# A new order of work for a two-layer block on one core, with every scaling of the K and Q features on GpSimd

## The chip, the core and the metric

The kernel runs on one core of a Trainium2 chip. The core has five engines with a queue of their own each: TensorE (PE in the profile; its weight loads are PEld), VectorE (DVE), ScalarE (ACT), GpSimd (POOL) and SyncE (SP), which here only issues transfers. An engine takes its instructions strictly in the order of its queue, and waits at an instruction until the semaphores that it names have come. The metric is the time of one execution in microseconds (us); less is better.

## The reference

The input x has 2048 tokens of 640 numbers. Two residual layers follow each other.

```python
h  = x + A(layernorm(x))
h2 = h + B(layernorm(h))
# A: 32 heads of 20
q, k, v = split(x @ wqkv)
phi(t)  = concat(softmax(t @ w_phi[h]), softmax(-(t @ w_phi[h])))     # 40 features
kv, z   = sum_s phi_k[s] v[s]^T,  sum_s phi_k[s]
o       = phi_q @ kv / (phi_q . z + 1e-6)
A       = o @ wo
# B: F = 1536
B       = ((x @ w_gate) * (x @ w_up)) @ w_down
```

So layer A is a linear attention: all tokens' K features must have been summed (kv and z) before the first token's numerator can be formed.

## The kernel before

The tokens lie in 16 tiles of 128. Every step of every tile is an operation with a name, a key, an engine and, for a tile of a pool, the slots that it takes. All this stands in the table PLAN (lines 48 to 142), one entry `name:key:choice:slots` per operation. `arrange` sorts each engine's operations by key, and that order is the engine's queue; the keys are used for nothing else. The choice picks the engine where an operation has two (0 the first, 1 the second). `emit` then works out which earlier operations each one has to wait for. Nothing is decided while the kernel runs, so the order of each queue is the table's.

The steps, with their names (t is the tile) and lines:

- Start: GpSimd fills constants (gl, gla, glb: a mask GL, lines 325 to 336; id0 and id1: the identity, 324 and 327; eps, va1, phz, ekz, rqz, Sz, mk0 to mk2). TensorE runs ten products of zeros, warm0 to warm9 (365). Ph0 to Ph2 (374) spread w_phi over the heads. WT0 to WT4 (386) turn the K weights on TensorE, WTe copies them, F1_0 to F1_4 (405) fold w_phi into them and Fe1 copies the result; the Q weights come turned by transfers (wqt) and are folded as F0 and Fe0. The loads are named x0, x1, x2, ... (x, some two tiles at a time), wk, wv, wo, wg, wu, wd.
- First layer norm: L1s and L1a on VectorE (422 to 425) give the mean and variance, L1l and L1e on ScalarE (430, 433) the factor, L1n (437) a bias for those tiles that ScalarE normalises, xn (445, 447) the normalised tile on VectorE or ScalarE. xt turns it: tiles 0 to 3 on TensorE (456) with a copy xte, the others by a transfer on SP (465).
- V, K and Q (476): ten products of 320 (or 300 and 340) columns into two banks of PSUM, 16 tiles each. Ve copies V out (245). For K, Kx (488) takes exp of both signs on ScalarE, Ks (492) sums each group of 20 on VectorE, Kr and Ke (495, 497) form the reciprocals on ScalarE, Kn (512) scales the 1280 features by them, and KV (520) adds the tile to the sums kv and z on TensorE, eleven products.
- For Q, Qx (545, 547) takes the exponentials, Qs (550) the sums, Qr (553), Qb (557) and Qe (560) form the ratio of the two sums of a head, Qn (564) scales half of the features, 660 columns, and qT (569) turns the tile by a transfer on SP.
- After the last KV, KVe0 and KVe1 on VectorE (527) copy kv and z out under a mask. Then for each tile N (582) forms numerator and denominator on TensorE, dd, rd and o (593, 596, 599) divide on VectorE, oT (603) turns o by a transfer, O (609) multiplies by wo, h (615) adds x, hc (623, 624) centres the result, L2q (626), L2v (630) and L2r (633) form the second layer norm's factor, and hT (637) turns the tile.
- Layer B goes by five groups of 2, 4, 4, 4 and 2 tiles (0 to 4; group 4 is the last two tiles). U_b_f_0 and U_b_f_1 (652) are the gate and up products of the f-th 128 columns, five products each; g (657) copies the gate on ScalarE, u (660) multiplies on VectorE; D (671) is the down projection, y (683) scales and adds h, and w (685) stores. The last tile's D is cut into three parts of 320, 192 and 128 columns.

Kn and Qn, the scalings, and Qb may run on GpSimd (choice 0) or on VectorE (choice 1). This is how Kn is written:

```python
G.op("pool", "Kn%d" % t, lambda e, eng, ek=ek, sr=sr: e.tensor_tensor(
    out=T["ek"][:, ek.slots[0], 0:2 * D].rearrange("p (h f) -> p h f", f=DH),
    in0=T["ek"][:, ek.slots[0], 0:2 * D].rearrange("p (h f) -> p h f", f=DH),
    in1=T["SR"][:, sr.slots[0], 1, :].unsqueeze(2).to_broadcast([P, 2 * H, DH]), op=ALU.mult),
    pool_c(1280), LP, [ek, sr], [ek], kk, alts=[("dve", dve_c(1280), LD)])
```

Of the kernel before, what the change touches and what calls it, by code (L numbers as in the profile page):

```python
# [48 lines left out]
gl0:0.78 gla4:0.942 gla1:1.084 glb1:1.313 gla0:1.452 gla3:1.594 gla2:1.736 glb2:1.965 va1:2.104 eps:2.934 zero:0.91 warm0:1.239 warm1:1.665 warm2:2.091  # L49
warm3:2.517 w5:0.78:1 x0:0.78:1 Ph1:2.585:1 glb4:2.964 ekz:3.103 warm4:2.943 L1s0:3.188 L1a0:4.098 x1:1.26 L1s1:4.207 wk0:1.74:1 L1l0:4.331 L1e0:4.657  # L50
xn0:4.994::0 warm5:3.369 wk2:2.22:1 id0:3.337 id1:3.575 warm6:3.795 warm7:4.221 WT0:4.647::0 glb3:3.82 WTe0:5.506:1 warm8:5.266::1 warm9:5.481 xt0:5.696::1
WT2:5.974::2 L1a1:5.914 L1l1:6.147 L1e1:6.473 xte0:6.173:1 Ph2:4.048 glb0:4.642 Ph0:4.87 F1_0:6.391::3 Fe1_0:6.909:1 wk3:2.7 WT3:6.71::5 WTe3:7.492:1 wk1:3.18
WT1:7.128::6 x2:3.66 wk4:4.14:1 x3:4.62:1 xn1:6.711::1 xt1:7.545::7 xte1:8.078 wv2:5.1:1 x6:5.58 WTe2:7.223:1 F1_2:7.824::0 Fe1_2:8.662:1 wv0:6.06:1
WT4:8.143::3 x4:6.54 WTe1:7.747 F1_1:8.559::4 Fe1_1:9.245 F1_3:8.879::6 Fe1_3:9.829 L1s2:8.155 wv1:7.02 K0_0:9.422::0 WTe4:8.942:1 F1_4:9.694::2 L1s3:9.35
L1a2:10.137 L1a3:10.26 K1_0:10.012::4 wv3:7.5 K1_1:10.284 K1_2:10.555 K1_3:10.825 V0_0:11.097::6 Fe1_4:10.414:1 L1s6:10.369 x10:7.98 L1s4:11.25 wv4:8.46:1
K1_4:11.367 L1l2:10.998 L1e2:11.323 Kx1_0:11.838::0 Kx1_1:12.421 L1a6:12.037 L1n2:11.604 K0_1:11.639 K0_2:11.909 K0_3:12.181 K0_4:12.451 Kx0_0:13.005::1
L1s7:12.146 V1_0:12.723::2 wqt4:8.94 V0_1:12.993 L1n3:11.828 V0_2:13.264 xn3:12.933::2 V0_3:13.536 wqt0:10.25 xn2:13.589:1:3 xt3:13.806::4 V1_1:14.085
V1_2:14.357 L1s5:13.445 V0_4:14.627 L1a4:14.232 x8:11.56 V1_3:14.899 Kx0_1:14.395 L1a7:14.341 L1a5:14.45 L1l4:14.979 L1e4:15.305 x14:15.398:1 xte3:14.559:1
Ve0:15.877::0 L1s11:14.967 xt2:15.169::5 xte2:16.462 V3:15.448::0 L1n5:15.754:1 xn5:15.908::0 xt5:16.533 L1n6:15.585 L1n4:15.809 V1_4:16.805 Ve1:17.274::1
xn4:16.42::1 xt4:17.843 Ks0:16.932::0 K3:17.076::6 L1s9:18.325 K2:18.431::4 wqt2:19.153 Kr0:18.444 Ke0:18.735 Ve3:18.881::2 L1a11:19.112 L1n7:16.032  # L60
xn7:19.465:1:2 xt7:20.463 Kx3_0:20.27::2 Kx3_1:20.854 L1a9:19.235 Ks1:19.344::1 Kr1:21.438 Ke1:21.729 Kx2_0:21.875::3 Kx2_1:22.459 L1s10:20.737 xn6:21.524::3
xt6:22.149 V2:19.788::2 K5:21.143::0 Kx5_0:23.043::4 Kx5_1:23.627 L1s8:22.036 V4:22.5::6 Ve2:24.211::3 L1a10:22.823 Ks2:23.195::2 Kr2:24.795 L1a8:24.588
K4:23.855::4 Ve4:24.941::4 L1l8:25.525 L1e8:25.851 Kn0:19.069 KV0:25.212::0,1 Ks3:24.697::3 Kn1:22.063 KV1:25.544 V7:25.878::2 K6:27.233::6 wqt3:23.459
Kx4_0:25.944::1 L1n9:26.131 xn9:26.433::0 L1n8:26.355 xn8:26.945::1 Kr3:26.528 Kx4_1:26.674 V6:28.59::4 wqt1:24.769 Ke2:27.258 Ve7:27.433::5 wg1:26.079
Ke3:28.017 Kx6_0:28.79::0 wo0:26.559 x12:27.039 F0_1:29.945::2 phz:26.579 Kn2:27.592 Kx6_1:29.373 xt9:27.519 Sz:29.905 Kn3:30.084 Ve6:30.145::6 Ks5:27.457::0
Kr5:30.73 L1s15:28.85 L1n11:29.637:1 xn11:29.791::2 Ke5:31.02 K7:30.265::6 KV2:31.62 rqz:32.397 Ks6:30.303::1 Kn5:32.434 Fe0_1:31.166 Ks4:31.696::2
Kx7_0:32.151::3 V5:31.953::4 Kx7_1:32.736 L1s14:33.089 L1a15:33.876 L1s13:33.985 xt8:28.829 Ve5:33.51::7 wg2:30.139 F0_3:33.309::2 L1a14:34.772 L1n10:34.881:1
xn10:35.035::3 KV3:33.629 L1s12:35.547 L1a12:36.457 Kr4:34.093 Ke4:34.385 Kn4:34.747 Fe0_3:34.531 Kr6:35.114 V8:33.962::6 Ve8:35.517::0 K9:35.318::4
F0_0:36.673::2 Kx9_0:36.873::2 Kx9_1:37.458 Ke6:38.041 wd0:30.619 K8:36.992::6 F0_2:38.349::4 L1a13:36.566 Fe0_2:38.865 Fe0_0:37.191:1 L1l12:39.45 L1e12:39.776
L1n15:40.056 KV4:38.667 Ks7:37.931::3 Kx8_0:39.868::1 wg0:31.099 F0_4:39.001::2 L1n14:40.014:1 Fe0_4:40.059:1 KV5:39.319 xt11:31.579 Kx8_1:40.453 L1n13:40.798:1  # L70
K11:39.653::4 Kx11_0:41.209::4 Kr7:41.792 Kx11_1:41.938 xn13:40.953::0 Ke7:42.523 Q0_0:41.008::2 wd2:32.889 Q3:41.281::6 wu2:33.369 Qx3_0:42.846::0 Qx3_1:43.456
L1n12:41.465:1 Kn6:40.279 xt10:35.66 wg4:36.97 Ks8:41.51::0 Kr8:44.066 Kn7:42.856 Ke8:44.356 Q0_1:42.648 Q0_2:42.919 Q0_3:43.191 Q0_4:43.464 xn15:42.903::1
wu4:37.45 xt15:43.528 wo2:44.502:1 wg3:44.837 KV6:43.736 V9:44.069::4 Q1_0:45.425::6 wu0:45.318 Q1_1:45.697 Q1_2:45.968 xt13:45.797 Ks9:43.414::2 Kr9:44.983
Kn8:45.169 xn14:44.807::2 Qx0_0:45.129::1 Qx0_1:45.739 wu1:47.108 Qs3:45.319 Ke9:46.349 Kn9:47.483 Q1_3:46.24 Q1_4:46.513 Qx1_0:46.983::2 Ks11:46.755::1
KV7:46.785 Ve9:47.593::1 xn12:48.148::3 xt12:48.773 Qx1_1:48.176 Qs1:48.971 Kr11:48.786 Q9:47.117::2 Qs0:50.407 Qx9_0:48.932::3 Qx9_1:49.542 KV8:48.484
K10:48.818::4 Kx10_0:50.373::0 Kx10_1:50.958 Ks10:51.842::3 xt14:50.083 Qr0:51.959::0 Qb0:52.303 K15:50.173::6 Kx15_0:52.105::3 KV9:51.529 Qr1:52.69::1
Qb1:53.033 Qs9:53.234 Kx15_1:52.836 Qe1:53.419 mk0:53.233 Ke11:53.538 wu3:51.392 wd1:51.873 V10:51.862::2 Qn1:53.727 Ve10:53.684::3 Kr10:54.269 Kn11:54.992
V11:53.218::4 Ve11:54.775::2 Ks15:54.669::0 K13:54.575::6 Qr9:55.358::2 Qb9:57.304 qT1:55.062::0 Qe0:55.505 Qr3:55.623::3 Qb3:56.062:1 Ke10:55.77 Kn10:56.163:1
Kr15:56.181 Kx13_0:56.328::1 Kx13_1:56.911 Ks13:58.33::2 Ke15:57.495 K12:55.931::2 Kx12_0:57.642::2 Kx12_1:58.225 Kn15:57.83 Qn0:59.722:1 Q2:57.286::4
Qx2_0:58.852::4 Qx2_1:59.462 qT0:60.7::1 Q4:58.654::6 Kr13:60.072 Ke13:60.362 Qe3:60.508 Qn3:60.816 qT3:62.191::2 Qx4_0:60.627::5 Qx4_1:61.237 Qs2:60.572  # L80
KV10:60.02 Qs4:62.032 Qr2:62.126::1 Qb2:62.469 V12:60.353::2 Ve12:62.272::4 Ks12:63.468::3 Qe2:62.855 Qe9:62.974 Qn2:64.861:1 K14:61.709::4 Qn9:63.282
qT9:64.617::3 Kx14_0:63.266::0 Kx14_1:63.849 Qr4:64.433::0 Q13:63.066::6 Qx13_0:64.63::2 Qx13_1:65.24 Kr12:65.85 Ke12:66.141 Kn13:64.546 Q5:64.433::2
Ks14:65.71::1 Qx5_0:66.287::1 Qx5_1:66.897 V14:65.799::4 Ve14:67.507::7 Qb4:66.859 Qe4:68.091 Kr14:68.21 Ke14:68.501 qT2:66.55::4 Qs5:67.692 Qr5:69.246::3
Kn12:67.058 V13:67.156::6 Ve13:69.391::6 Q10:68.511::2 Qn4:69.127:1 Qx10_0:70.076::0 KV11:69.879 Qs13:69.978 V15:70.212::4 Kn14:69.371 Qx10_1:70.686 Qs10:71.481
KV12:71.567 KV13:71.9 Ve15:71.767::5 KV14:72.234 KV15:72.567 mk1:71.684 mk2:72.029 KVe0:73.097 Q6:72.9::6 qT4:70.106::5 KVe1:73.686 N1:74.266::2 Qb5:72.299
Qe5:72.575 Qn5:72.882 Qr13:72.694::2 Qb13:74.147 Qe13:74.421 dd1:74.797::0 rd1:75.013 Qr10:74.54::1 N3:74.6::4 qT5:74.79::0 o1:75.415::0 oT1:76.343::0
Qn13:74.728 qT13:77.653::2 Qx6_0:74.686::3 Qx6_1:75.296 dd3:76.227::0 rd3:76.442 o3:76.844::1 oT3:79.142::1 Q7:74.933::0 Qx7_0:76.498::4 Qx7_1:77.108 Qs7:77.903
N0:76.299::6 Q11:76.632::2 dd0:79.338::0 rd0:79.552 o0:79.956::2 Qx11_0:78.198::5 Qx11_1:78.808 Qr7:79.456::0 Qb7:79.799 Qe7:80.075 N2:77.999::4 oT0:80.882::2
Qb10:80.766:1 Q14:78.332::0 Qx14_0:80.194::1 Qx14_1:80.803 Q8:79.7::2 Qx8_0:81.862::2 Qx8_1:82.472 dd2:80.867::0 rd2:81.082 o2:81.484::0 O1:81.067::6 h1:82.624
Qe10:83.082 Qn7:80.382 qT7:82.192::1 N9:82.424::0 dd9:83.424::0 oT2:83.683::3 hc1:83.558::1 Q12:82.757::4 Qx12_0:86.403::4 Qx12_1:87.013 L2q1:87.623 rd9:83.638  # L90
o9:84.041::1 Qn10:83.389 N5:84.124::2 dd5:84.853::0 rd5:85.067 o5:85.471::2 O0:84.457::6 h0:86.281 L2q0:88.483 hc0:87.216:1:0 oT9:84.993::0 hT1:86.302
O3:85.816::0 hT0:87.79 N4:87.174::2 dd4:87.704::0 Q15:87.507::6 h3:87.811 rd4:88.611 qT10:89.099::4 Qs6:88.894 Qr6:90.448::3 Qb6:90.791 O2:88.874::4 h2:90.43
# [820 lines left out]
```

## Time and profile before

| | |
|---|---|
| time before, median of three runs | 275.81 us (275.66 to 277.15) |
| the profiled execution | 275.82 us |
| its span in the profile | 274.1 us |
| TensorE busy | 265.9 us, 97% |
| VectorE busy | 173.0 us, 63% |
| ScalarE busy | 121.3 us, 44% |
| GpSimd busy | 67.9 us, 25% |
| granted TensorE clock | 1.00 of full speed |

In the first 80 us VectorE is busy for 73.8 us, and GpSimd does 54.2 of its 67.9 us there. Matmuls are pipelined and the profile models their ends, so that a group starts 0.16 us before the modelled end of the one in front of it when nothing keeps it waiting; a wait shows as a later start. The number behind L is the line of the kernel. In a row of the timeline the bracket holds the time in which the engine was idle in front of the instruction, and the operation that ended it. In the chain that ended last, each row is one stretch of work on the path to the last instruction.

### The profile page before, as it was taken

To read this page: it belongs to the slowest core of one execution; us is meant where nothing else is said; L and a number is where in the kernel's file an instruction comes from. 1 tells how busy PE (TensorE), PEld (TensorE's weight loads), DVE (VectorE), ACT (ScalarE), POOL (GpSimd) and SP (SyncE) were. 2 spreads that over 40 slices of the span, in tenths; PEclk is the share of its full clock that TensorE was granted. 3 is DMA by queue.
4 is the path that set the end of the run, shared out by engine and by line. 5 is a ranking of instruction groups with operands and counts; after the bars stand their busy time and mean duration, and the time that the engine had idled before them with its cause. 6 is when DMAs were issued, how large, how long until landed. Compare 5 with 4: busy or idle time off the path is not lost.

```text
span 274.1 us, 5191 instructions
## 1 busy us (share of the span) xinstructions
PE 265.9 (97%) x2103; PEld 176.5 (64%) x2103; DVE 173.0 (63%) x310; ACT 121.3 (44%) x299; POOL 67.9 (25%) x88
## 2 busy tenths in 40 slices
PE   7999999999879999999999999999999999999996
PEld 2777787777556688856666676757544466544674
DVE  4999989999989998785984445231323331344314
ACT  2989878998747565322336144111213020004000
POOL 7026959498942104232000000000000000000000
PEclk9999999999999999999999999999999999999999
DMA  6985999967558979567436400027000000010003
GB/s 183 315 178 110 232 330 216 246 197 118 94 82 157 145 159 139 114 124 144 58 72 128 42 0 2 6 66 122 0 29 4 0 0 26 25 60 0 26 0 103
DMA packets 66600, 27.76 MB, mean 101 GB/s; under 512 B 57744, under 2 KB 65296, under 8 KB 66576
## 3 DMA queue, kind: packets, MB, share of 16 engines
q1 hardware_dynamic: 65760, 26.45, 46.1%
q10 hardware_dynamic: 816, 0.98, 1.3%
q8 instruction: 16, 0.26, 0.4%
q14 instruction: 8, 0.07, 0.1%
HBM read 11.00 MB, written 2.62 MB: 50 GB/s over the span
## 4 chain that ended last, share of the span: by engine, by line
PE 81%; DVE 13%; ACT 3%; POOL 1%; issue 1%; DVEq 0%; ACTq 0%; POOLq 0%
PE ps L652 38%; PE ps L671 19%; PE ps L476 13%; PE ps L609 7%; DVE S L550 5%; DVE SR L492 3%; DVE ph L564 2%; PE ps L582 2%; ACT ph L545 1%; PE ps L520 1%; PE ps L405 1%; DVE RQ L557 1%; DVE o L599 1%; DVE ek L512 1%; ACT Wp L245 0%
## 5 line engine op out<-in xcount | busy, mean ns | idle before, releaser
L652 PE MATMUL ps<-xnT,Wgu 128*128 128x512 bf16 (+1 forms) x600 | 107.5, 336 | 0.0
L652 PEld LDWEIGHTS ps<-xnT,Wgu 128*128 128x128 bf16 x600 | 58.3, 98 | 42.3 <-DVE ev L660 0.4
L476 PE MATMUL ps<-Wp,xnT 128*128 128x320 bf16 (+1 forms) x480 | 69.1, 299 | 0.7 <-DVE o L599 0.4
L657 ACT ACTIVATE gt<-ps 128x512 bf16<-128x512 f32 (+1 forms) x60 | 29.2, 510 | 90.6 <-PE ps L652 65.9
L660 DVE TENSOR_TENSOR ev<-ps,gt 128x512 bf16<-128x512 f32 (+1 forms) x60 | 33.3, 580 | 43.5 <-PE ps L652 26.8
L476 PEld LDWEIGHTS ps<-Wp,xnT 128*128 128x128 bf16 x480 | 45.0, 97 | 18.4 <-ACT ph L547 0.7
L671 PE MATMUL ps<-Wd,ev 128*128 128x320 bf16 (+2 forms) x396 | 54.0, 295 | 0.0
L671 PEld LDWEIGHTS ps<-Wd,ev 128*128 128x128 bf16 x396 | 38.0, 98 | 15.7 <-DVE ev L660 0.3
L683 DVE SCALAR_TENSOR_TENSOR Wp<-ps,rs,x_all 128x640 bf16<-128x640 f32 (+3 forms) x18 | 14.5, 808 | 41.2 <-PE ps L671 41.1
L512 POOL TENSOR_TENSOR ek<-ek,SR 128x1280 bf16<-128x1280 bf16 x15 | 36.1, 2418 | 4.2 <-ACT SR L497 4.2
L545 ACT ACTIVATE ph<-ps 128x600 bf16<-128x600 f32 x32 | 21.2, 676 | 6.5 <-PE ps L582 3.4
L550 DVE TENSOR_REDUCE S<-ph 128x66 f32<-128x1320 bf16 x16 | 23.9, 1512 | 0.3 <-ACT ph L547 0.2
L609 PE MATMUL ps<-Wo,Wp 128*128 128x320 bf16 x160 | 23.7, 299 | 0.2 <-ACT ph L547 0.2
L492 DVE TENSOR_REDUCE SR<-ek 128x64 f32<-128x1280 bf16 x16 | 23.4, 1470 | 0.2 <-ACT ek L488 0.2
L488 ACT ACTIVATE ek<-ps 128x640 bf16<-128x640 f32 x32 | 20.9, 699 | 1.8 <-PE ps L476 1.4
L564 POOL TENSOR_TENSOR ph<-ph,RQ 128x660 bf16<-128x660 bf16 x13 | 17.5, 1355 | 10.5 <-ACT RQ L560 10.3
L609 PEld LDWEIGHTS ps<-Wo,Wp 128*128 128x128 bf16 x160 | 15.3, 98 | 7.1 <-issue 0.7
L626 ACT ACTIVATE ek<-x_all,mv 128x640 bf16<-128x640 bf16 x16 | 13.2, 824 | 10.9 <-DVE x_all L615 10.7
L630 POOL TENSOR_SCALAR ln<-mv 128x1 f32<-128x1 f32 x11 | 2.1, 192 | 58.2 <-ACT ek L626 57.7
L615 DVE SCALAR_TENSOR_TENSOR x_all<-ps,x_all 128x640 bf16<-128x640 f32 x16 | 13.1, 819 | 4.5 <-PE ps L609 4.5
L599 DVE TENSOR_TENSOR o<-ps,sm 128x720 bf16<-128x720 f32 x16 | 14.4, 902 | 0.7
L245 ACT ACTIVATE ev<-ps 128x640 bf16<-128x640 f32 x16 | 11.4, 710 | 0.9 <-PE ps L476 0.4
(67 smaller groups left out, 172.3 us busy)
## 6 DMA issues: line engine op xcount, KB each, us to landing
out_dram<-Wp SPq DMA_DIRECT2D x15, 160.0 KB, 1.8
Wgu<-in_B_w_gate_dram SPq DMA_DIRECT2D x5, 384.0 KB, 5.0
Wd<-in_B_w_down_dram SPq DMA_DIRECT2D x4, 480.0 KB, 5.0
Wgu<-in_B_w_up_dram SPq DMA_DIRECT2D x5, 384.0 KB, 6.5
x_all<-in_A_x_dram SPq DMA_DIRECT2D x5, 320.0 KB, 5.5
ev<-in_A_wqkv_dram SPq DMA_DIRECT2D x5, 160.0 KB, 3.4
Wp<-in_A_wqkv_dram SPq DMA_DIRECT2D x5, 160.0 KB, 5.2
x_all<-in_A_x_dram SPq DMA_DIRECT2D x3, 160.0 KB, 3.8
```

Of the source, the lines that this page charges most:

```text
L476: ins = e.matmul(pb(b, hb)[:, 0:n1 - n0], lhsT=T["xnT"][:, NC - 1 - c, P * t:P * (t + 1)], rhs=T["Wp"][:, POS[kind], c, n0:n1], start=(c = ...
L488: G.op("act", "%sx%d_%d" % (nm, t, s), lambda e, s=s, b=b, ek=ek: e.activation(out=T["ek"][:, ek.slots[0], 0:2 * D].rearrange("p (b h s f) ...
L492: G.op("dve", "%ss%d" % (nm, t), lambda e, ek=ek, sr=sr: e.tensor_reduce(out=T["SR"][:, sr.slots[0], 0, :], in_=T["ek"][:, ek.slots[0], 0: ...
L512: G.op("pool", "Kn%d" % t, lambda e, eng, ek=ek, sr=sr: e.tensor_tensor(out=T["ek"][:, ek.slots[0], 0:2 * D].rearrange("p (h f) -> p h f", ...
L545: e.activation(out=v[:, 0:10].rearrange("p (b g) j f -> p b g j f", b=2), in_=pp(b, 0, 300).rearrange("p b (g j f) -> p b g j f", j=3, f=D ...
L550: G.op("dve", "Qs%d" % t, lambda e, t=t, ph=ph: e.tensor_reduce(out=T["S"][:, t, 0:66].rearrange("p (g k) -> p g k", k=6), in_=pv(ph).rear ...
L564: return e.tensor_tensor(out=v, in0=v, in1=T["RQ"][:, rq.slots[0], 1, 0:33].rearrange("p (g j) -> p g j", j=3).unsqueeze(3).to_broadcast([ ...
L609: ins = e.matmul(pb(b, hb)[:, 0:320], lhsT=T["oT"][:, oT.slots[0], c, :], rhs=T["Wo"][:, c, 320 * hb:320 * (hb + 1)], start=(c == 0), stop ...
L652: ins = e.matmul(pb(b)[:, 0:n], lhsT=T["Wgu"][:, gu, c, P * ft:P * (ft + 1)], rhs=T["xnT"][:, NC - 1 - c, o0:o0 + n], start=(c == 0), stop ...
L657: G.op("act", "g%d_%d" % (bi, ft), lambda e, pg=pg, gt=gt, n=n: e.activation(out=T["gt"][:, gt.slots[0], 0:n], in_=pb(pg)[:, 0:n], func=AF ...
L660: o_ = G.op("dve", "u%d_%d" % (bi, ft), lambda e, pu=pu, gt=gt, hh=hh, ft=ft, n=n: e.tensor_tensor(out=T["hh"][:, hh.slots[0], ft, 0:n], i ...
L671: ins = e.matmul(pb(b, hb)[:, 0:w], lhsT=T["hh"][:, hh.slots[0], ft, P * tt:P * (tt + 1)], rhs=T["Wd"][:, ft, c0 + w * hb:c0 + w * (hb + 1 ...
```

## The change

Only the table PLAN differs. No operation is added or taken away: both tables have the same 1018 entries. The ten products of zeros and the four tiles (0 to 3) whose x is turned on TensorE are in both. What differs are the order of every queue, many slots, and the engine of some operations:

- Kn10, Qn0, Qn2, Qn4, Qb3, Qb10, Qb11 and Qb14 go from VectorE to GpSimd, so that all Kn, Qn and Qb are there.
- The biases L1n5, L1n10, L1n12, L1n13 and L1n14 go from VectorE to GpSimd, L1n7 the other way. Ph1 goes from VectorE to GpSimd, in front of the second half of the identity (id1).
- xn3, xn4, xn6, xn8 and xn10 go from VectorE to ScalarE, xn2 the other way. The copies Ve2, Ve10, Ve11, Ve13, Fe0_2, Fe0_3 go from ScalarE to VectorE, Fe0_0 and Fe0_4 the other way; WTe0, WTe1, WTe2 and xte0 go to ScalarE, WTe3, xte1, xte2 and Fe1_2 to VectorE. Some hc and L2v of the second layer norm change engines too.
- On SP, x1 and x0 now stand first, w5 goes to ScalarE's queue. wu1 and wg4 (384 KB each) and x12 are loaded early, in front of x8, x10 and wqt0. wd0 and wd2 are issued from ScalarE, x0, x14 and wo2 no longer are.
- On TensorE, warm8 and warm9 stand with the other eight; the order of the V, K and Q groups is another (Q7 comes before the first numerator N1, Q2 and Q4 and others change places), and the products of groups 0, 1 and 4 of layer B are mixed otherwise with the numerators and O. Kn15 is the last K scaling instead of the fourth from the end.
- The end of the queue is nearly the same: D14, D10, D12, D11, D13, D15_1.

The entries that the text speaks of, one to a line (all others change their keys too):

```diff
-Kn10:56.163:1
+Kn10:55.445
-Qn0:59.722:1
+Qn0:57.957
-Qn2:64.861:1
+Qn2:69.554
-Qn4:69.127:1
+Qn4:65.312
-Qb3:56.062:1
+Qb3:47.539
...
-Kn15:57.83
+Kn15:70.819
-L1n10:34.881:1
+L1n10:24.5
-Ph1:2.585:1
+Ph1:4.778
-id1:3.575
+id1:5.17
...
-xn4:16.42::1
+xn4:18.632:1:1
-xn6:21.524::3
+xn6:17.39:1:0
-Ve10:53.684::3
+Ve10:51.962:1:3
-Ve11:54.775::2
+Ve11:57.97:1:2
...
-x8:11.56
+x8:11.21
-x10:7.98
+x10:11.69
-wu1:47.108
+wu1:8.94
-wg4:36.97
+wg4:9.42
...
-Q6:72.9::6
+Q6:69.966::6
-Q7:74.933::0
+Q7:74.354::0
-N1:74.266::2
+N1:75.721::6
```

## The prediction

> **What bounds the kernel now.** I read the page first (engine shares, slices), then TensorE's timeline, the chain that ended last, and GpSimd's timeline against VectorE's. In each timeline row the columns are start, duration, what it is, and in brackets the idle time in front and who ended it.
>
> ```profile
> PE 265.9 (97%) x2103; PEld 176.5 (64%) x2103; DVE 173.0 (63%) x310; ACT 121.3 (44%) x299; POOL 67.9 (25%) x88
> ```
> TensorE is busy for 97% of 274.1 us, so a new order can win only what TensorE waits. Its timeline, from 66 us on:
> ```profile
> 65.81 3.70 PE L476 MATMUL ps<-Wp,xnT 128*128 128x300 bf16 x26
> 69.68 1.54 PE L476 MATMUL ps<-Wp,xnT 128*128 128x300 bf16 x10 [0.17 <-ACT ph L547]
> ...
> 74.42 0.51 PE L520 MATMUL ps<-ev,ek 128*128 128x63 bf16 x11 [0.50 <-POOL ek L512]
> 75.31 0.51 PE L520 MATMUL ps<-ev,ek 128*128 128x63 bf16 x11 [0.39 <-ACT ev L245]
> 75.67 1.53 PE L476 MATMUL ps<-Wp,xnT 128*128 128x300 bf16 x10
> 78.83 0.85 PE L582 MATMUL ps<-KVm,scratch 128*128 128x63 bf16 x22 [1.63 <-DVE KVm L527]
> ```
> Between 10.03 us (K0's first product) and 69.5 nothing waits: each group starts 0.16 before the last one's modelled end. Then come waits in front of Q10, KV13, KV14, KV15, N1, Q12 and O2: 0.17, 0.16, 0.50, 0.39, 1.63, 0.43 and 0.23, with the lost overlap 4.6 us. After O2 there is none. A count agrees: with 1.36 us per ten-product group, 0.33 per K'V or numerator, 1.08 and 0.545 per five gate/up products, 3.26 per down projection (pieces of the chain), the work after 10.03 is 256.6; the last product ends at 271.51, so 4.9 us are lost.
>
> Who makes TensorE late? The chain, 49.8 to 78.8 us, is VectorE throughout:
> ```profile
> 54.17 1.44 DVE S L550
> 55.61 1.39 DVE SR L492
> 57.00 1.27 DVE RQ L557
> 58.27 1.50 DVE ek L512
> 59.77 1.40 DVE SR L492
> 61.16 1.52 DVE ph L564
> 62.68 2.87 DVE S L550 x2
> 65.56 1.39 DVE SR L492
> 66.95 2.69 DVE ph L564
> 69.64 1.40 DVE SR L492
> 71.04 1.43 DVE S L550
> 72.47 2.60 DVE ph L564
> ```
> These are reductions (L492, L550), four scalings (L512, L564: Kn10 1.50, Qn0 1.52, Qn2 2.69, Qn4 2.60) and one small subtraction (L557: Qb3 1.27), the five together 9.6 us. They are long because of GpSimd:
> ```profile
> 58.70 3.28 POOL L512 TENSOR_TENSOR ek<-ek,SR 128x1280 bf16<-128x1280 bf16 x1 [0.28 <-ACT SR L497]
> 61.95 1.91 POOL L564 TENSOR_TENSOR ph<-ph,RQ 128x660 bf16<-128x660 bf16 x1
> ...
> 66.58 2.36 POOL L512 TENSOR_TENSOR ek<-ek,SR 128x1280 bf16<-128x1280 bf16 x1
> ```
> Qn2 on VectorE, the 2.69 at 66.95, ends at 69.64, 0.7 after GpSimd's scaling (Kn13) that ends at 68.94, so it did most of its work only then; Kn15 on GpSimd takes 3.28 instead of 2.36 beside Kn10. Two-input scalings on the two engines exclude each other; the reductions keep 1.4 beside any GpSimd work.
>
> **Head, to 10 us.** K0_0 starts after the same work in both orders (ten zero products, five W-turns, two x-turns, four folds). The identity now stands behind Ph1, which is new on GpSimd. Start to start from before's rows: fills and selects 0.15 (0.27 when dependent), ph's fills 0.77, Ph2 and Ph0 0.61, Ph1 about 0.4 (between Qb's 0.24 at 32 columns and 0.66 at 280). The identity ends near 6.1 (before 4.28), WT2 starts 6.15 (WT0 5.37). But x1 and x0 lead SP's queue and land 2.5 to 2.9 after issue, as before: at 3.5 and 4.1; two statistics (0.9 each) and ScalarE's pair (0.5) later xn1 ends near 5.9 and xn0 near 6.5 (before 8.06 and 6.34). The copies then chain on ScalarE at 0.6 each: WTe2 7.35, WTe0 7.95, xte0 8.55, WTe1 9.15, Fe1_0 9.75. K0_0 starts at 9.85; wv0 is issued 0.5 earlier and lands near 10.5. Change: -0.1, bounds -0.4 (nothing waits for wv0) and +0.5 (wv0 as late as before's 10.98).
>
> **Loads, 14 to 28 us.** wu1 and wg4 (384 KB each) stand in front of x8, x10 and wqt0. At 1.1 us each (the slices run at 230 to 390 GB/s) x8 lands near 18.1, x10 near 19.2 (before 17.46 and 13.68). VectorE reaches their statistics at 18.3 and 19.1; xt5 lands about 21.4 and K5 is due at 21.7. Nothing, up to 0.5.
>
> **VectorE, 50 to 79 us.** Gone: the 9.6. Added: Ve10, Ve11, Ve13 at 0.74 (a cast from PSUM, 0.82 less overlap) and Qs6 1.44, together 3.7. Net -5.9, more than the waits of 4.6. ScalarE loses four V copies (4 x 0.6) and takes xn3, 4, 6, 8 and 10 but not xn2 (net four x 0.82), so +0.9 by 79 us; it was busy 35.6 of the 40 us from 10 to 50 and 17.2 of 19 from 50 to 69, so it must be followed joint by joint (below).
>
> **GpSimd.** Added: Kn10 2.32, three Qn at 1.27, Qb3 0.20 and five L1n at 0.24 less L1n7: about 7.3. Gone: the blocked time of Kn15, Qn3, Qb4 and mk1 (0.9, 0.6, 0.6, 0.6). From Kn0 to Kn15 it has 15 x 2.32 + 6 x 1.27 + 6 x 0.2 + 1.9 of small ones = 45.5 us. Kn0 waits in the queue behind L1n10, L1n9 and L1n8, these for L1e8, that for x8's and x10's statistics: start near 26.2. Never starved, Kn15 would end at 71.7; followed through ScalarE's and VectorE's queues (it waits 1.4 for Ke4, some 0.8 elsewhere), at 73.9. KV15 is due at 74.7.
>
> **Does something else bind?** I laid TensorE's groups end to end from 9.85 and compared each group's start with its releasers, each on its own queue at before's durations. Margins up to N1 are mostly 0.2 to 1 us, but at five places 0.15 or less: KV0 (due 28.6) on Kn0 (28.5), KV6 (45.85) on Kn6 (45.75), V10 (50.6) on Qx9 (50.45), KV15 (74.7) on Ve15 (74.6), N1 (76.4) on KVe0 (76.4). I take 0.25 us for them, 0.05 each; all of them late by 0.3 would be 1.5. N1 falls at 76.5 with Q7 already done; before it was 78.83 with Q7 (1.37) still to come, a gain of 3.7. Behind N1 VectorE binds: o1, dd0, rd0, dd3, rd3, o0 (0.84 each o, 0.64 each dd and rd) put o0 at 80.45 while Q8 is due at 80.1: +0.4. o3, Qs7 and o2 end at 84.2 while Q12 is due 83.9: +0.4. N7 waits 0.15 for Qx12. From KVe1 (75.5) to u0_11 VectorE has 31.4 us of work (ten dd-rd-o at 1.48, seven h at 0.74, four Qs at 1.44, twelve u0 at 0.34, KVe and small ones 1.5); D1_0 is due at 111.8, so it fits into 36.3, with 0.3 to 1 us of room at each joint. Later margins are larger; SP's turns land 1 us or more before need. The tail (D13, D15_1, y15_1, w15_1) is the same.
>
> Sum: -0.1 head, -4.6 old waits, +0.95 new waits, +0.25 thin joints = -3.5. The profiled execution is 275.82, 1.72 beyond its span, and the median is 275.81: 272.3 us.
>
> A rule speaks against it. The Trainium skill (GPSIMD Engine Reference, § 4.1 Engine selection) gives two-input elementwise work to VectorE, since GpSimd is about twice as slow. The row agrees in part (2.42 against 1.58 at 1280 columns); at 660 columns GpSimd's 1.31 beats VectorE's blocked 2.35. By that rule GpSimd's queue would bind, which is the slower rival below (278.3); by the rows the sum stays 272.3.
>
> **Rivals.** *Slower: GpSimd's queue takes over.* Place: Kn0 behind L1e8, then 45.5 us in order to Kn15, for which KV15, KVe0 and all numerators wait. Each us of Kn15's end beyond 74.7 costs one, so the gain of 3.5 is gone at 78.2 and 277.2 is reached at 79.6. For: 0.8 of room after 47 us of chained work. Against: it needs 6 us more than my count; every scaling alone takes 2.36 or 1.31. Say Kn15 at 80.7: 278.3. 0.13.
>
> *The waits come back.* The denser half (group 0's gate/up products end 10 us earlier beside the last Q features) turns VectorE's 31.4 of 36.3 us into waits, or x10 and xt5 are late. At eight joints 0.4 each: 275.5. For: 0.3 us margins; against: SP, GpSimd and TensorE are free there. 0.14.
>
> *Full gain.* No new wait: -0.4 - 4.9 = 270.5. Against: Q8 and Q12 behind o0 and o2. 0.13.
>
> *Nothing changes*, because the scalings were hidden anyway: 275.8. The chain holds them, so 0.02, within the second rival's side.
>
> **Chances.** Forecast (271.2 to 273.9) 0.58, full gain 0.13, waits back 0.14, no change 0.02, GpSimd bound 0.13. Half a per cent, 1.4 us, is about what a measurement can tell from no change: faster means below 274.4, slower above 277.2. Faster: 0.58 + 0.13 + 0.04 of the waits' rival = 0.75; same 0.10 + 0.02 = 0.12; slower 0.13. Range for 8 in 10: from 270.6 (bound of the full gain) to 275.5.
>
> **What would show it.** Right: no scaling on VectorE, all GpSimd Kn at 2.36 and Qn at 1.31; N1 near 76.5; TensorE's waits from 69 to 95 near 1 us instead of 4.6, those left before Q8 and Q12 behind L599; the last product near 268. Wrong: waits of K'V products for L512 (GpSimd), of K5 for a transfer, or waits after 95 us.

## The result, and the profile after

The changed kernel takes 272.35 us (median of four runs, 272.27 to 272.55); the kernel before took 275.74 on the same chip (275.60 to 277.15). The ratio is 0.9867, 95% interval 0.9834 to 0.9899. The profiled execution is the one of 272.55, its span 270.8.

The page of the changed kernel: engine shares first, then two of its costliest groups (busy us, mean ns of one, idle time in front and what ended it).

```profile
PE 266.0 (98%) x2103; PEld 177.1 (65%) x2103; DVE 161.6 (60%) x295; ACT 123.8 (46%) x304; POOL 72.8 (27%) x98
...
L512 POOL TENSOR_TENSOR ek<-ek,SR 128x1280 bf16<-128x1280 bf16 x16 | 37.5, 2357 | 4.0 <-ACT SR L497 3.9
...
L564 POOL TENSOR_TENSOR ph<-ph,RQ 128x660 bf16<-128x660 bf16 x16 | 20.8, 1306 | 10.2 <-ACT RQ L560 10.0
```

TensorE's busy time is what it was (266.0, before 265.9). What went is waiting: the last product ends at 268.28 us instead of 271.51. VectorE lost 11.4 us of busy time. GpSimd gained only 4.9, although five of the operations that it took over had cost VectorE 9.6: nothing holds its scalings up any more, and all sixteen of K now take 2.36, all sixteen of Q 1.31.

TensorE's timeline, the stretch that was shown of before, with the start of the head in the first row (start, duration, line, idle time in front):

```profile
6.03 1.17 PE L386 MATMUL ps<-ident,ev 128*128 128x128 bf16 x10 [0.33 <-POOL ident L327]
...
73.97 1.54 PE L520 MATMUL ps<-ev,ek 128*128 128x63 bf16 x44
75.36 1.53 PE L476 MATMUL ps<-Wp,xnT 128*128 128x300 bf16 x10
76.73 0.84 PE L582 MATMUL ps<-KVm,scratch 128*128 128x63 bf16 x22
...
84.50 1.54 PE L476 MATMUL ps<-Wp,xnT 128*128 128x300 bf16 x10 [0.20 <-DVE o L599]
...
93.89 0.51 PE L582 MATMUL ps<-KVm,scratch 128*128 128x63 bf16 x11 [0.38 <-ACT ph L547]
```

The four K'V sums now run as one group of 44 products, without the waits of 0.16, 0.50 and 0.39 that cut them before, and N1 follows at 76.73 (78.83 before) without its wait of 1.63. What is left in the brackets are a wait in front of Q12 on VectorE's o2 and one in front of N7 on ScalarE.

The chain shows the same exchange. Between 50 and 77 us it was VectorE throughout; now it is TensorE's own work:

```profile
53.02 6.80 PE ps L476 x50
59.83 0.34 PE ps L520 x11
60.16 12.28 PE ps L476 x90
72.44 0.34 PE ps L520 x11
72.77 1.36 PE ps L476 x10
74.13 1.38 PE ps L520 x44
```

VectorE's timeline says why. It has holes where it was packed:

```profile
53.59 1.48 DVE L492 TENSOR_REDUCE SR<-ek 128x64 f32<-128x1280 bf16 x1
55.75 1.49 DVE L492 TENSOR_REDUCE SR<-ek 128x64 f32<-128x1280 bf16 x1 [0.69 <-ACT ek L488]
57.51 1.49 DVE L492 TENSOR_REDUCE SR<-ek 128x64 f32<-128x1280 bf16 x1 [0.27 <-ACT ek L488]
...
70.43 2.96 DVE L550 TENSOR_REDUCE S<-ph 128x66 f32<-128x1320 bf16 x2 [1.73 <-ACT ph L547]
```

In each hole VectorE waits for ScalarE's exponentials. Two of the three had waited for TensorE's products in their turn: those behind the hole of 0.69 for 0.30 us, those behind the hole of 1.73 through the V copy in front of them, which had waited 0.82. In front of the hole of 0.27 ScalarE was simply busy. TensorE, which has no wait in this stretch, leads, and VectorE follows.

### The profile page after: what moved, and what is told of

Read it like the earlier page. It is cut to its first block, busy times and chain, and to the rows that moved or that the text cites. A ratio compares the mean times of both kernels' runs of the same rounds, so it can differ in the third digit from the quotient of the medians.

```text
span 270.8 us, 5184 instructions
## 1 busy us (share of the span) xinstructions
PE 266.0 (98%) x2103; PEld 177.1 (65%) x2103; DVE 161.6 (60%) x295; ACT 123.8 (46%) x304; POOL 72.8 (27%) x98
## 4 chain that ended last, share of the span: by engine, by line
PE 90%; DVE 3%; DMA 3%; ACT 2%; POOL 1%; issue 0%; SPq 0%; DVEq 0%; POOLq 0%
PE ps L652 38%; PE ps L476 22%; PE ps L671 19%; PE ps L609 6%; PE ps L520 2%; DMA scratch<-ph 2%; PE ps L582 1%; DVE o L599 1%; PE ps L405 1%; DMA w<-in_A_w_phi_dram 1%; DVE sm L596 1%; ACT scratch L245 1%; POOL Phi L374 1%; DVE S L550 1%; ACT ph L545 0%; ACT ek L626 0%
## 5 line engine op out<-in xcount | busy, mean ns | idle before, releaser
L671 PE MATMUL ps<-Wd,ev 128*128 128x320 bf16 (+2 forms) x396 | 53.3, 295 | 0.0
L512 POOL TENSOR_TENSOR ek<-ek,SR 128x1280 bf16<-128x1280 bf16 x16 | 37.5, 2357 | 4.0 <-ACT SR L497 3.9
L630 POOL TENSOR_SCALAR ln<-mv 128x1 f32<-128x1 f32 x8 | 1.5, 190 | 89.3 <-ACT ek L626 88.9
L564 POOL TENSOR_TENSOR ph<-ph,RQ 128x660 bf16<-128x660 bf16 x16 | 20.8, 1306 | 10.2 <-ACT RQ L560 10.0
L624 ACT ACTIVATE xn<-x_all,mv 128x640 bf16<-128x640 bf16 x10 | 8.2, 825 | 9.5 <-DVE x_all L615 9.5
```

Of the source, the lines that this page charges most:

```text
L564: return e.tensor_tensor(out=v, in0=v, in1=T["RQ"][:, rq.slots[0], 1, 0:33].rearrange("p (g j) -> p g j", j=3).unsqueeze(3).to_broadcast([ ...
L671: ins = e.matmul(pb(b, hb)[:, 0:w], lhsT=T["hh"][:, hh.slots[0], ft, P * tt:P * (tt + 1)], rhs=T["Wd"][:, ft, c0 + w * hb:c0 + w * (hb + 1 ...
```

## The experiments

The theory on trial was that of the prediction: TensorE is the bound, VectorE between 50 and 79 us made it late, and taking the five operations (Kn10, Qn0, Qn2, Qn4, Qb3) off VectorE is what frees it. The rivals were that the new order does it by itself, and that GpSimd takes over as the bound. Every experiment edits only PLAN, except for the two that add work.

### The new order without the move, and the move without the new order

```diff
 # five_back_on_vector, against the changed kernel
-Kn10:55.445 Qn0:57.957 Qn2:69.554 Qn4:65.312 Qb3:47.539
+Kn10:55.445:1 Qn0:57.957:1 Qn2:69.554:1 Qn4:65.312:1 Qb3:47.539:1
 # five_moved_alone, against the kernel before
-Kn10:56.163:1 Qn0:59.722:1 Qn2:64.861:1 Qn4:69.127:1 Qb3:56.062:1
+Kn10:56.163 Qn0:59.722 Qn2:64.861 Qn4:69.127 Qb3:56.062
```

> The new order, with Kn10, Qn0, Qn2, Qn4 and Qb3 back on VectorE and everything else as in the changed kernel. Theory (these five made VectorE the bound): in the changed kernel VectorE is idle for about 4.5 us between 50 and 76 us; beside GpSimd the five cost about 7 (they took 9.6 in the old order, 4 if nothing kept them off), so N1 is late by 2.5 and the time is about 274.9 us, with scalings of 1.6 to 2.8 us on VectorE. Rival (the order is what wins, the engine of the scalings is beside the point): 272.6 us or less.

> The old order, with only Kn10, Qn0, Qn2, Qn4 and Qb3 moved from VectorE to GpSimd. Theory: VectorE's chain of 49.8 to 78.8 us loses 9.6 us and TensorE most of its waits of 4.6; Q7 still stands behind N1, so about 1 us stays: about 272.9 us. Rival (the order wins): 275 us or more. Rival (GpSimd takes over): K'V products wait for L512 and the time is 276 us or more.

The first took 275.49 us (ratio to before 0.9984, 0.9961 to 1.0006): the new order alone wins nothing that can be measured. TensorE's timeline of it has two waits that the changed kernel doesn't have:

```profile
52.89 1.53 PE L476 MATMUL ps<-Wp,xnT 128*128 128x320 bf16 x10 [1.25 <-ACT ph L547]
63.65 12.44 PE L476 MATMUL ps<-Wp,xnT 128*128 128x300 bf16 x90 [1.42 <-DVE ev L245]
```

VectorE's timeline of the same kernel shows what is late:

```profile
49.25 2.01 DVE L557 TENSOR_TENSOR RQ<-RQ 128x32 f32<-128x32 f32 x1
...
59.23 1.48 DVE L512 TENSOR_TENSOR ek<-ek,SR 128x1280 bf16<-128x1280 bf16 x1
60.62 1.48 DVE L492 TENSOR_REDUCE SR<-ek 128x64 f32<-128x1280 bf16 x1
62.02 0.84 DVE L564 TENSOR_TENSOR ph<-ph,RQ 128x660 bf16<-128x660 bf16 x1
62.77 0.82 DVE L245 CAST ev<-ps 128x640 bf16<-128x640 f32 x1
```

The subtraction Qb3, 32 columns, is held 2.01 us, until GpSimd's Kn8 has ended at 51.22; Qe3 then stands in ScalarE's queue in front of Qx9, and V10 waits 1.25 us for the PSUM slot that Qx9 frees. The second wait is for the copy Ve11 (L245), which now stands behind Kn10 and Qn0. Against the expectation of 1.6 to 2.8 us the four scalings were hardly held here: they took 1.48, 0.84, 0.83 and 1.13 us, since three of them began while GpSimd had no scaling in hand (in front of its Kn13 it was idle for 3.77 us). They cost by their own length, ahead of the copy.

The second took 277.49 us, slower than before (ratio 1.0061, 1.0043 to 1.0079). I had expected 272.9, and the rival came true instead: in the old order GpSimd does take over. TensorE's timeline has KV14 waiting for Kn14:

```profile
77.56 0.85 PE L520 MATMUL ps<-ev,ek 128*128 128x63 bf16 x22 [2.73 <-POOL ek L512]
```

GpSimd's timeline of this kernel has two long idle stretches ahead of that:

```profile
40.89 0.26 POOL L437 TENSOR_SCALAR nb<-mv,rs 128x1 f32<-128x1 f32 x1 [3.02 <-ACT rs L433]
...
53.26 0.24 POOL L557 TENSOR_TENSOR RQ<-RQ 128x32 f32<-128x32 f32 x1 [2.53 <-ACT RQ L553]
```

In the old order GpSimd stands idle for 3.02 us until ScalarE has the layer norm factor of tiles 12 to 15, and for 2.53 in front of Qb0 (the kernel before has the same two, 2.92 and 2.53), and after that, but for gaps of 0.50, 0.41 and 0.46, works through to Kn14. The table by stretch (stretch, its length, then busy us of PE, PEld, DVE, ACT, POOL, each with its count, then the granted clock, the busy share of the DMA engines and GB/s) has the sum for 26 to 76 us, of this kernel:

```profile
26.00:76.00 50.00, 47.83 (x485) 35.21 (x483) 41.29 (x49) 42.55 (x117) 41.66 (x34) 1.00 0.86 200
```

and of the changed one:

```profile
26.00:76.00 50.00, 50.00 (x523) 37.72 (x522) 44.90 (x50) 43.79 (x122) 46.95 (x39) 1.00 0.86 194
```

The new order keeps GpSimd busy for 46.95 of these 50 us, the old one for 41.66. So neither part of the change is worth anything alone: the old order doesn't keep GpSimd fed, and the new one, as it stands, can't bear the five on VectorE. Whether another order could (with Qb3 in front of Kn8 and Ve11 in front of Kn10, say) was not tried.

### Filling one of GpSimd's idle stretches in the old order

```diff
 # against five_moved_alone
-Ke11:53.538 Kn11:54.992
+Ke11:48.8 Kn11:49.0
```

> The old order with the five operations on GpSimd, and Kn11 (with its exponential Ke11) put into the 2.5 us in which GpSimd stood idle in front of Qb0. Theory (in the old order the moved work failed only because GpSimd's queue has an idle stretch just before its chain of 15 us to Kn14): KV14's wait of 2.73 falls below 0.6, the profiled execution is 274.1 (276.5 less 2.4), the median near 274.5. Rival (the old order fails for another cause, ScalarE's or VectorE's joints): another wait of about the same size takes its place and the median stays at 277 or above.

It took 276.33 us (ratio to before 1.0009, 0.9992 to 1.0027). Neither expectation fits as written. The idle time in front of Qb0 did fall from 2.53 to 0.22, but 0.87 of it came back in front of Qb3, and KV14 starts 1.45 us earlier, at 76.11. Its wait is still 2.73: the waits of 0.80 and 0.20 that TensorE had ahead of it are gone (1.3 with the lost overlap), K0_0 had started 0.28 earlier, and so TensorE reaches KV14 earlier by about as much. The other idle stretch, 3.00 us at 37.8, is still there. Against the move alone the median fell by 1.16 us, by the ratios to before by 1.4. Two of its ten executions kept a full clock, with 275.37 and 275.92 us; the other eight had a mean of 0.993 or 0.994 and 276.2 to 276.7. So the idle stretch is part of the cause, and filling one of the two isn't enough.

### One part of the five at a time

```diff
 # only_qb3_back, against the changed kernel
-Qb3:47.539
+Qb3:47.539:1
 # only_scalings_back, against the changed kernel
-Kn10:55.445 Qn0:57.957 Qn2:69.554 Qn4:65.312
+Kn10:55.445:1 Qn0:57.957:1 Qn2:69.554:1 Qn4:65.312:1
```

> The changed kernel with one operation, the small subtraction Qb3, back on VectorE. Theory (a 32-column operation on VectorE is held until GpSimd's scaling ends, so Qe3 comes late and holds ScalarE's queue): Qb3 takes about 2.0 us instead of 0.25, Q projection behind Qx9 waits about 1.2, 273.5. Rival (only the four large scalings count): 272.4.

> The changed kernel with the four scalings Kn10, Qn0, Qn2, Qn4 back on VectorE and Qb3 left on GpSimd. Theory: TensorE waits 1.4 us for the V copy Ve11 that stands behind Kn10 and Qn0 in VectorE's queue, and some 0.5 later: 274.2. Rival (the parts don't add, the small subtraction alone made the loss of 3.1): 272.6.

They took 273.74 (ratio to before 0.9925, 0.9897 to 0.9952) and 273.90 us (0.9930, 0.9902 to 0.9957): 1.4 and 1.55 above the changed kernel's 272.35, and together 2.95, where all five cost 3.14. (Worked out from the ratios to before it is 1.6 and 1.7, and 3.2 for all five.) Each shows its own wait of the two and not the other. TensorE's timeline with Qb3 back:

```profile
52.41 1.53 PE L476 MATMUL ps<-Wp,xnT 128*128 128x320 bf16 x10 [1.25 <-ACT ph L547]
```

and with the four scalings back:

```profile
61.47 12.44 PE L476 MATMUL ps<-Wp,xnT 128*128 128x300 bf16 x90 [1.42 <-DVE ev L245]
```

An operation that takes 0.24 us on GpSimd costs as much on VectorE as four large ones, since it is held there for 2.01 us, until a scaling on GpSimd has ended.

### How much room GpSimd has in the new order

```diff
 # pool_dose_2 (range 2) and pool_dose_4 (range 4): products on GpSimd ahead of Kn15 whose result nothing uses
+    for k in range(2):
+        G.op("pool", "pad%d" % k, lambda e: e.tensor_tensor(
+            out=T["Phi"][:, :, :].rearrange("p j f -> p (j f)"), in0=T["Phi"][:, :, :].rearrange("p j f -> p (j f)"),
+            in1=T["Phi"][:, :, :].rearrange("p j f -> p (j f)"), op=ALU.mult), 1.4, LP, phi_b, phi_b, 70.8 + 0.001 * k)
```

> The changed kernel with two more GpSimd products of 720 columns (on w_phi's spread copy, which nothing reads any more) in front of Kn15, 1.4 us each. Theory (GpSimd is 0.8 us from being the bound at KV15): Kn15 ends 2.8 later, at 77.0 instead of 74.2, and KV15 waits 2.0 us: 272.35 + 2.0 = 274.3 us. If GpSimd had room, 272.4 us.

> The same with four such products, 5.6 us. Theory: Kn15 ends at 79.8 and KV15 waits 4.8 us: 277.1 us, twice the dose and a step of 2.8 over the smaller one, which is the slower rival of the prediction made on purpose. If GpSimd had room, 272.4 us.

They took 274.61 (0.9986, 0.9965 to 1.0007) and 279.45 us (1.0138, 1.0122 to 1.0154). KV15 waits 1.93 and 4.86 us for Kn15, so the third and fourth product add 2.93 to the wait, and by the same measure the first two use up 1.0 of room before it begins. The prediction's 0.8 of room before KV15 is about right. The time of the larger dose is 4.84 above the smaller, 1.9 more than the added wait. The missing part is the clock. The table by stretch of the larger dose has it in the column behind POOL:

```profile
74.00:78.00 4.00, 1.50 (x37) 1.27 (x35) 1.53 (x1) 1.22 (x3) 3.84 (x4) 1.00 0.34 63
78.00:82.00 4.00, 1.64 (x16) 1.18 (x17) 0.85 (x2) 0.37 (x2) 3.66 (x4) 0.54 0.02 4
82.00:86.00 4.00, 4.00 (x37) 2.89 (x36) 1.62 (x5) 1.66 (x5) 1.92 (x3) 0.61 0.09 19
86.00:90.00 4.00, 3.91 (x47) 2.77 (x45) 3.56 (x7) 1.76 (x5) 0.00 (x0) 1.00 0.97 182
```

After the idle time TensorE runs at about half its clock for some 5 us (0.54 and 0.61), and the first ten-product group after KV15 takes 2.84 us instead of 1.54.

### The forecast's joints, mended

What was left of waits in the changed kernel is 1.7 us by the count of the prediction (268.28 less 9.96, the start of K0_0, less 256.6 of work). If these are real waits of the bounding engine, taking them away must show in the time.

```diff
 # mended, against the changed kernel
-id1:5.17   V0_0:10.1::4  x12:7.02  wu1:8.94  wg4:9.42  Qx12_1:91.205
+id1:2.345  V0_0:10.7::4  x12:9.6   wu1:31.48 wg4:31.49 Qx12_1:89.6
 # mended_2: the same, but
+wu1:50.0   wg4:50.1
 # loads_after_turns: only wu1:50.0 and wg4:50.1
```

> The changed kernel with three of its joints mended: the identity is finished right after its fill instead of behind Ph1, with V0_0 behind K0_2 and x12 behind wg4 on SP (0.4 us earlier at K0_0); wu1 and wg4 issued behind the tokens' loads x8, x10 and the turns up to xt11 (removes VectorE's wait of 0.46 for x8, so that Kn0 keeps up with KV0); Qx12_1 ahead of Qr6, L2q0 and Qe6 on ScalarE (removes N7's wait of 0.38, 0.54 with the lost overlap). Theory (TensorE is the bound and these are its waits): 272.35 - 0.4 - 0.5 = 271.4. Rival (thin joints behind the head, KV0, Q8 and Q12, take it back): 272.0 to 272.4.

> The mended version with one thing changed: wu1 and wg4 are issued behind the last of the tokens' turns (xt14) instead of ahead of xt10, xt15, xt13, where they made K13 wait 1.29 us for xt13. Theory (that wait, 1.45 with the lost overlap, is all that took the gain back): 272.5 - 1.45 = 271.1, no wait at K13, the last product near 267.1. Rival (the earlier head meets the thin joints at V10, KV15 or N1 instead): 272.0 or more, with a wait of 0.4 or more at one of them.

> The changed kernel with only wu1 and wg4 moved on SP from ahead of x8, x10 to behind xt14. The prediction took the earlier place at nothing, up to 0.5. Theory (x8, x10 and xt5 had room behind wu1 and wg4): x8 lands near 17.5 instead of 19.3, VectorE's wait of 0.46 goes, TensorE gains nothing: 272.3. Rival (the two transfers cost the full 0.5): 271.8.

The first, at 272.51 us (ratio to before 0.9873, 0.9841 to 0.9904), gained nothing. K0_0 starts at 9.47, 0.49 earlier, and N7's wait is gone, but a new wait, of which neither expectation spoke, took it all back: the two transfers, put in front of the later turns on SP, made xt13 late (with them behind the last turn, next, the wait is gone). TensorE's timeline at K13:

```profile
53.57 6.97 PE L476 MATMUL ps<-Wp,xnT 128*128 128x320 bf16 x50 [1.29 <-DMA xnT<-xn]
```

With the transfers behind the last turn, 271.54 us (0.9829, 0.9802 to 0.9856; 270.81 to 271.88). Its profiled execution, 270.81, has one bracket left in TensorE's timeline from 5 to 100 us:

```profile
83.43 1.54 PE L476 MATMUL ps<-Wp,xnT 128*128 128x300 bf16 x10 [0.20 <-DVE o L599]
```

The last product ends at 266.54, and from K0_0 on 0.85 is lost instead of 1.7. K0_0 starts at 9.09, 0.38 earlier than in the first version with the same head; most of that is chance, since the turn WT0 took 0.45 us in this profile and 0.69 to 0.72 in those of the changed kernel and the first version. That this version beats the changed kernel is seen best against the third, which ran beside it and takes 272.36 (0.9862, 0.9839 to 0.9885), as the changed kernel does: 0.8 us by the medians, and the slowest of its five executions is faster than the fastest of the other's four (271.88 against 272.24). The third also shows that the early wu1 and wg4 cost nothing. With them moved x8 lands at 15.44 us instead of 19.31 and VectorE's wait of 0.46 for it is gone, but no TensorE wait depended on it, and the time stays.

### ScalarE's room

```diff
 # four_copies_back, against the changed kernel
-Ve2:23.18:1:3 Ve10:51.962:1:3 Ve11:57.97:1:2 Ve13:63.527:1:6
+Ve2:23.18::3  Ve10:51.962::3  Ve11:57.97::2  Ve13:63.527::6
```

> The changed kernel with the V copies Ve2, Ve10, Ve11, Ve13 on ScalarE instead of VectorE. Theory (ScalarE, busy 37.4 of 40 us from 10 to 50, is as near to its limit as GpSimd, and its exponentials release GpSimd's scalings): each copy puts 0.6 us ahead of a Kx, Qx or Ke, GpSimd's room of 0.8 before KV15 is used up, TensorE waits about 0.9 in all: 273.2. Rival (ScalarE has room): 272.4.

It took 273.03 us (0.9887, 0.9859 to 0.9914), 0.7 above the changed kernel. The theory of a nearly full ScalarE holds, though not by the path it named: KV15 doesn't wait. KV0 waits for Kn0 (0.27 with the lost overlap), which stands behind ScalarE's L1e8 and so behind Ve2, and Q5 waits for Kx14, 0.7 later in ScalarE's queue because of Ve11:

```profile
65.90 7.00 PE L476 MATMUL ps<-Wp,xnT 128*128 128x300 bf16 x50 [0.17 <-ACT ek L488]
```

So the four copies on VectorE, 3.0 us of the work that the change puts there, earn 0.7 of its 3.4.

## Why the prediction was right

**What bounds.** TensorE did, and the gain is the waits of 4.6 us between 69 and 95 less those that are left. The experiments on Qb3 and the scalings show that in the new order VectorE's delays are what the move takes away. Only half of it goes the way that the prediction read, by an operation held by GpSimd's scaling: that is Qb3. The four scalings, read there at 1.5 to 2.7 us because of GpSimd, took 0.83 to 1.48 on VectorE in the new order and still cost as much as Qb3, by standing in front of Ve11. That the hold made the waits in the old order is read from the chain, not shown by a run: the move alone took VectorE out of the way there, and GpSimd was late instead.

**Head.** Forecast K0_0 at 9.85, -0.1; it started at 9.96 (10.03 before). The identity ended at 5.89 (6.1 forecast), WT2 started at 6.04 (6.15). The products V0_0 and V0_3 wait 0.14 each for wv0 and wv3, which landed at 10.65 and 14.60; that was inside the bound of +0.5 but not in the sum. These 0.28 us are about what the last product came later than forecast (268.28 against 271.51 less 3.5, so 268.0).

**Loads.** x8 landed at 19.31 (18.1 forecast), x10 at 20.20 (19.2), xt5 at 21.38 (21.4), and K5 started without a wait: nothing, as forecast, and with a run of its own that shows it. The size was off: in the run without the two in front of it x8 landed at 15.44, so they cost it 3.9 us, 1.9 each, and not the 1.1 that I took from the slices' rates.

**VectorE and ScalarE.** VectorE was busy for 23.83 of the 29 us from 50 to 79 instead of 28.77, 4.9 less against a forecast of 5.9. ScalarE rose from 35.57 to 37.39 of the 40 us from 10 to 50 and fell by 1.3 in the 30 us behind, 0.6 more in all by 80 us against a forecast of 0.9.

**GpSimd.** Forecast: Kn0 at 26.2, a wait of 1.4 for Ke4, Kn15's end at 73.9. Measured: 26.34, 1.65 and 74.21. The doses confirm the room. That this room belongs to the new order alone, and that the moves without it make the kernel slower, I had not seen; the prediction costed the move in the new order only, which was enough for the sum. The slower rival's rule that each us of Kn15's end beyond 74.7 costs one was too low: from the smaller dose to the larger 2.93 us of it cost 4.84, for the clock.

**Joints.** I took 0.25 for five thin ones; KV0, KV6, V10, KV15 and N1 all started without a wait above 0.03. Q8 and Q12 behind o0 and o2 were forecast at 0.4 each and cost 0.25 and 0.36. N7, forecast at 0.15, cost 0.54 with its lost overlap: the turn qT7 took 5.3 us from issue (86.03) to landing (91.33), so Qx12_0, which needs the slot that this turn frees, waited 0.71 for it, and Qr6, L2q0 and Qe6 stand between it and Qx12_1. The step that failed here is "SP's turns land 1 us or more before need". The mended version, which puts Qx12_1 in front of them, has no wait at N7. U0_2_0 lost 0.13 more. Together 1.3 us instead of 1.2, by other shares: thin joints nothing, N7 more. That the two sums agree is luck. After 95 us there is no wait, as forecast.

**Sum.** The last product came 3.23 us earlier, the profiled execution is 3.27 and the median 3.4 below before's; forecast 3.5. The mechanism was right; that the median meets the forecast of 272.3 within 0.05 is luck, for the profiled execution, on which the sum was worked out, was 0.25 above it.

**The rule against it.** By the Trainium skill (GPSIMD Engine Reference, § 4.1 Engine selection) the five belong on VectorE. In this kernel the runs decide otherwise: with them on VectorE it takes 275.49 us, on GpSimd 272.35. For Qb3, half of the difference, what explains it agrees with another page of the Trainium skill (SBUF — State Buffer, § Who interferes with whom: of a VectorE instruction with two SBUF inputs and a GpSimd instruction that reads SBUF, the second to issue waits for the first): Qb3's 2.01 us against 0.24 on GpSimd is such a case.

## What to carry to other kernels

Where two engines hinder each other, cost a move by what the operation takes at its place, beside what runs there, not by its size: 32 columns cost 1.4 us here, as much as four scalings of 660 to 1280. A move to an engine with a low busy share still needs an order that feeds it: look for that engine's idle stretches ahead of the point where its last result is due, since the same move made this kernel 1.7 us slower in one order (0.9 in the executions with a full clock) and 3.1 faster in the other. And when mending a wait by moving a transfer, follow what the queue issues next at the new place.

## What the runs showed of the hardware

I had not expected the clock to fall within a kernel that is 97% busy. After TensorE's idle time of 4.86 us the granted clock was half for some 5 us in the profile (0.50 in the stretches of 1 us from 80 to 85), and all four timed executions had a mean clock of 0.988. Waits of 2.73 us show both: the profile of the move alone has such a wait and a clock of 1.00 behind it, that of the version with Kn11 early has the same wait and 0.64 from 78 to 82 us. There the clock was still full at the end of the wait, at 76.1, and was half from about 77.5 to 80.9 (0.75 from 77 to 78 us, 0.50 to 80, 0.54 to 81). Five of eight executions of the first had a mean clock of 0.994 and took 1.3 us more on average than the other three; eight of ten of the second had 0.993 or 0.994 and took 0.8 more than the other two. In the smaller dose, with 1.93 us, it was four of ten, and 1.65 us. With waits of up to 1.63 us in the profile (the kernel before has that one) no execution shows less than 0.999. The Trainium skill (TensorE: Matmul & The Clock Gate, Part 1) has the clock fall to half after an idle window of about 3.4 us that runs free of the kernel; the half agrees, but here waits shorter than that in the profile went with it in part of the executions. Why some and not others isn't settled: only one execution of each kernel has a profile, and so a measured wait. So on this kernel a wait of TensorE of about 2 us or more may cost 0.8 to 1.9 us on top of itself, and that was about half of the loss of the move alone.
